# Seven block products for eight in the second quarter of the last network's first half

## The chip, the cores and the metric

The kernel runs on one core of a Trainium2 chip. The metric is the time of one execution in device microseconds, here the median of three. The engines are named as in the profile: PE is TensorE's matrix multiplication (PEld its weight load), DVE is VectorE, ACT is ScalarE, POOL is GpSimd, SP is SyncE.

## The reference

Attention over windows of 128 positions with a linear bias gives x (1152 tokens of 512 elements). Four networks of experts follow, weighted by domain probabilities, and then one network of 2048 hidden elements with a squared relu:

```python
scores = scale * np.matmul(q, k.transpose(0, 1, 3, 2))      # masked to a window of 128, with bias
attn_out = softmax(scores) @ v
x = attn_out, heads side by side                            # 1152 x 512

for e in range(4):                                          # w1: 4 x 512 x 1024, w2: 4 x 1024 x 512
    h = np.maximum(x @ w1[e], 0.0)
    out += p[:, e:e + 1] * (h @ w2[e])

x = out
h = np.maximum(x @ w_in, 0.0)                               # w_in: 512 x 2048
return h * h @ w_out                                        # w_out: 2048 x 512
```

## The kernel before

Every product of two f32 matrices is computed from high and low parts (xh, xl for x; wh, wl for weights): three matmuls, high by high, high by low and low by high. TensorE does all the products, the other engines make the parts.

The kernel counts six networks. Numbers 0 to 3 are the experts; the last network is cut into two halves of 1024 hidden elements, number 4 (`E`) and number 5. Each of them has four groups g of 256 hidden elements, and each group two weight loads: index 2 x (4 e + g) for the first matrix, plus one for the second. Two groups make what is called a quarter below: r = 0 is network 4's first quarter, r = 2 its second.

Work goes in items, in the order of the list `items`. There are two sorts. A **single** item (lines 1155 and 1186 of the code, matmuls on L939 and L1166) takes one of three chunks of 384 tokens and one tile of 128 hidden elements: 12 matmuls of 384 columns for gemm1. Four tiles make a stage of 48. Their gemm2 takes 36 matmuls per chunk, three row tiles of 12. A **pair** item (`gemm1_pair`, matmuls on L1053; gemm2 on L1131) takes a pair of chunks of tokens (2 x 256 or 2 x 320, `PAIRS`) and a group of 256 hidden elements, cuts x, weights and result into two by two blocks and computes the four blocks of the result from seven block products in place of eight, so with 42 matmuls. That needs sums of blocks: of weights (`w_forms`: wsum on L356, ha, hs, la, ls; 11 POOL operations, where hi and lo parts need 4) and of x (`x_forms`: t1, t2, m4, t3 for each pair of chunks, 14 DVE operations on L975 and 4 roundings on ACT, L1006, in two work tiles fxwork). The sums t3 go back into the place of xh and xl, so they wait until single items have read those (`x_free`).

A pair's seven products use three accumulators, pa, pb, pc. Group 2 writes pb, DVE adds it to the copy p1 into u2, group 5 goes on in pb and gives u3; c12, c21 and c22 follow, then the squared relu r (for networks 4 and 5) and its parts hmem. For single items of these networks the squared relu is r on L1152 (DVE, after ACT's L1151), hmem on L1153 and POOL's remainder on L500.

Networks 1 to 3 are pairs throughout; network 4 is single throughout; network 5 is pairs. Network 4 begins by turning the experts' sum into the new x by transposes (`to_x2`, L1201), tile by tile.

The last network's weights come as 64-bit numbers and are converted during the middle networks (`convert`): each load is taken in two halves, and a half is an ACT absolute value (L271), a DVE clamp (L277) and shift (L284) and two DVE joins (L291) on tiles wconv and wraw, then a store to memory (L251) and the next load (L239), both on ACT's queue. In `convert` these are a list of closures; each returns False if it isn't its turn.

A planner sets the order on each engine. `fill` is called between groups of matmuls with the time that passes; it takes up to three steps of `xbg` (sums of x), up to three of `conv`, and as many weight steps of `bg` as `pace` allows. `clock` holds, per engine, how far its assumed work reaches; a step with no room is put off. `spent` adds an assumed duration, as 0.85 for a POOL operation of a weight form. The engines then run their lists strictly in order.

Of the kernel before, what the change touches and what calls it, by code (L numbers as in the profile page):

```python
# [130 lines left out]
def kernel(  # L131
# [14 lines left out]
    nc = tc.nc  # L146
# [76 lines left out]
    def convert():  # L223
# [10 lines left out]
        def load(j, eng):  # L234
            i, h = todo[j]
            src, nk, nf = w_src(*order[i])
            raw[j] = places[j % 2][0]
            m = nk // 2
            eng.dma_start(  # L239
                out=raw[j].rearrange("p (k f) t -> p k (f t)", k=m).bitcast(mybir.dt.int64),  # L240
                in_=src[:, h * m:(h + 1) * m, :],
            )
            at["raw", j] = clock["now"] + 7.0

        def swap(j):
# [9 lines left out]

        def reload(j):
            if not by(at["out", j]):
                return False
            load(j + 2, nc.scalar)

        def steps(j):
# [3 lines left out]
            def begin():  # L265
                if not (by(at["raw", j]) and by(at.get(("gone", j - 2), 0.0))):
                    return False
# [20 lines left out]
            def join(part, amount, op):  # L288
# [6 lines left out]
                at["out", j] = clock["DVE"] + 0.5  # L295
# [5 lines left out]
            if j + 2 < len(todo):  # L301
                ops.append(lambda: reload(j))
            if j:
                ops.insert(1, lambda: swap(j - 1))
            if j + 1 == len(todo):
                ops += [lambda: swap(j), lambda: (fxkeep.append(places[0]), fxkeep.append(places[1]),
                                                  free.append(buf))[-1]]
            return ops
# [29 lines left out]
    def w_forms(i):  # L338
# [30 lines left out]
        def part_lo(o, src):  # L369
# [4 lines left out]
            spent("POOL", 0.85)  # L374
# [8 lines left out]
        def done(o):  # L383
# [7 lines left out]
            spent("POOL", 0.85)  # L391
# [19 lines left out]
    def w_ops(i):  # L411
# [24 lines left out]
        def lo(o):  # L436
# [4 lines left out]
            spent("POOL", 0.85)  # L441
# [592 lines left out]
    def remainder(out, x, y, n, lag):  # L1034
# [4 lines left out]
        spent(eng, 0.15 + (0.0024 if eng == "POOL" else 0.0014) * n, lag)  # L1039
# [131 lines left out]
    def evac(e, ch, tiles, f=0, two=False):  # L1171
        c0 = PAIRS[ch][0] if two else chunks(e)[ch][0]
        for i, y in tiles:
            nt = c0 // P + i
            if e == 0 or (e == E and f < FT // 2):
# [3 lines left out]
            spent("ACT" if e == E and f < FT // 2 else "DVE", 0.74, 1.38 if two else 0.69)  # L1179
# [8 lines left out]
            elif e == E and f < FT // 2:  # L1188
                nc.scalar.activation(out=yt, in_=y, func=ACTF.Copy)
            elif e == E:  # L1190
                nc.vector.tensor_tensor(out=yt, in0=y, in1=yt, op=ALU.add)
# [40 lines left out]
    for e in range(1, NE):  # L1232
        for r in range(0, NQ, 2):
            if e == E:
# [97 lines left out]
    def fill(share, us, need=0.0):  # L1332
# [24 lines left out]
    def pace(it):  # L1357
# [8 lines left out]
        return max(most * step, len(bg) / 2)  # L1366
# [296 lines left out]
    fxwork, fxbuf, fxkeep, x_late, conv = [], [], [], [], []  # L1663
# [13 lines left out]
    def want(i):  # L1677

        clock["force"] = True
        while i not in ready:  # L1680
            bg_run()
            if i not in ready:
                loads()
                while wnext["load"] == wnext["ops"] and conv:
                    assert conv.pop(0)() is not False
                    loads()
# [4 lines left out]
    for it, (e, ch, f, two) in list(enumerate(items))[N1:]:  # L1691
# [8 lines left out]
        if e >= E and (ch or f):  # L1700
            run_x2("y")
        quota["n"] = pace(it)
# [6 lines left out]
        else:  # L1709
# [20 lines left out]
        if (e, f) in ((0, FT - 1), (E, FT - 1)) and not two:  # L1730
# [6 lines left out]
        last = not two and (e, ch, f) in ((0, len(CHUNKS0) - 1, FT - 1), (E, len(CHUNKS) - 1, FT - 1))  # L1737
# [37 lines left out]
```

## Time and profile before

| | |
|---|---|
| median of three runs | 669.87 us (669.85 to 670.09) |
| the profiled execution | 669.66 us |
| its span | 667.8 us |
| PE busy | 657.0 us (98%) |
| DVE, ACT, POOL busy | 477.3, 316.9, 388.7 us |

The span is the part of the execution between the first and the last instruction that the profiler saw; 1.86 us lie outside it. Times in the trace are microseconds from the span's start. A row of the timeline gives start, duration (the sum of both where it says x2), engine, line, operation, what is written and read, and in brackets the engine's idle time ahead of it with what ended it. Matmuls are pipelined: each row shows 0.28 us and more, and the next begins 0.12 us after it for 256 columns.

### The profile page before, as it was taken

Reading aid. Unit: us, or ns where it says so; the run is one execution under the profiler, and the core shown is the slowest. Engines: PE = TensorE matmul, PEld = TensorE weight load, DVE = VectorE, ACT = ScalarE, POOL = GpSimd, SP = SyncE. Lnnn points to the kernel's source line nnn. Section 1 sums busy time; section 2 is a strip of 40 time slices with the busy share of each in tenths; the row PEclk is TensorE's granted clock in tenths of the full one; section 3 lists DMA queues with packets and bytes.
Section 4 is the critical chain, followed back from the end, with each engine's and each line's share of the span. In section 5 each row is a group of like instructions: output and inputs, shape, how many; then the busy total and the mean of one; then the engine's idle time right before and its main releaser. Section 6 shows DMA issues by size and latency. Waiting matters only on the chain.

```text
span 667.8 us, 10929 instructions
## 1 busy us (share of the span) xinstructions
PE 657.0 (98%) x3892; PEld 586.9 (88%) x3892; DVE 477.3 (71%) x983; ACT 316.9 (47%) x765; POOL 388.7 (58%) x468
## 2 busy tenths in 40 slices
PE   8999999999999999999999999999999999999997
PEld 7788788889889899898989999898999999898996
DVE  5799997847878877777877876876668744545453
ACT  7898787623534433334343443333464534333120
POOL 4588886536957744653654554331458984856331
PEclk9999999999999999999999999999999999999999
DMA  9943232010413444344335245354122001100012
GB/s 239 260 116 83 66 84 62 11 64 31 158 32 111 141 143 121 117 128 152 116 127 158 79 147 170 118 166 147 60 95 79 1 1 63 64 1 1 0 64 79
DMA packets 44022, 64.42 MB, mean 96 GB/s; under 512 B 4160, under 2 KB 26176, under 8 KB 43968
## 3 DMA queue, kind: packets, MB, share of 16 engines
q1 hardware_dynamic: 32704, 39.35, 19.3%
q10 hardware_dynamic: 11264, 24.38, 12.2%
q8 instruction: 30, 0.49, 0.3%
q14 instruction: 24, 0.20, 0.1%
HBM read 52.97 MB, written 10.75 MB: 95 GB/s over the span
## 4 chain that ended last, share of the span: by engine, by line
PE 87%; DVE 5%; ACT 3%; POOL 2%; issue 1%; DMA 1%; SPq 0%; POOLq 0%
PE yacc L1131 29%; PE hps L1053 26%; PE yacc L1166 13%; PE hps L939 12%; PE xps L733 2%; PE tp L861 1%; POOL ts L849 1%; PE sc L813 1%; DVE ts L825 1%; DVE khl L500 1%; ACT ts L834 1%; DMA first<-in_qT_dram 1%; DVE pt L500 1%; PE xtp L1201 1%; DVE fxwork L975 1%
## 5 line engine op out<-in xcount | busy, mean ns | idle before, releaser
L1131 PE MATMUL yacc<-wh,hmem 128*128 128x512 f32 x576 | 183.7, 390 | 0.0
L500 POOL TENSOR_TENSOR wl<-wraw,wh 128x256 fp32r<-128x256 f32 (+1 forms) x107 | 103.8, 994 | 63.8 <-ACT wh L433 51.2
L1131 PEld LDWEIGHTS yacc<-wh,hmem 128*128 128x128 f32 x576 | 108.2, 188 | 21.7
L1131 PE MATMUL yacc<-wl,hmem 128*128 128x512 f32 x288 | 112.4, 390 | 0.0
L1166 PE MATMUL yacc<-wh,hmem 128*128 128x512 f32 x272 | 89.3, 393 | 0.0
L500 POOL TENSOR_TENSOR ls<-wsum,hs 128x256 fp32r<-128x256 f32 x64 | 54.5, 879 | 48.1 <-ACT hs L380 47.6
L1064 ACT ACTIVATE p<-hps 128x256 f32<-128x256 f32 (+1 forms) x64 | 26.2, 410 | 98.7 <-PE hps L1053 98.2
L939 PE MATMUL hps<-xh,wh 128*128 128x384 f32 (+1 forms) x208 | 66.8, 321 | 0.4 <-DVE xl L500 0.4
L939 PE MATMUL hps<-xh,wl 128*128 128x384 f32 (+1 forms) x208 | 65.5, 315 | 0.0
L939 PE MATMUL hps<-xl,wh 128*128 128x384 f32 (+1 forms) x208 | 65.4, 314 | 0.0
L1068 DVE TENSOR_TENSOR u<-hps,p 128x256 f32<-128x256 f32 (+1 forms) x64 | 29.1, 455 | 50.1 <-PE hps L1053 50.0
L1131 PEld LDWEIGHTS yacc<-wl,hmem 128*128 128x128 f32 x288 | 54.1, 188 | 10.0
L1166 PEld LDWEIGHTS yacc<-wh,hmem 128*128 128x128 f32 x272 | 51.0, 188 | 10.4
L291 DVE SCALAR_TENSOR_TENSOR wconv<-wraw,wconv 128x512 int32<-128x512 int32 x64 | 57.2, 893 | 1.3
L1088 ACT ACTIVATE hmem<-c 128x256 fp32r<-128x256 f32 (+1 forms) x72 | 31.0, 445 | 54.0 <-DVE c L1068 52.8
L500 POOL TENSOR_TENSOR la<-wraw,ha 128x256 fp32r<-128x256 f32 x48 | 44.4, 948 | 20.0 <-ACT ha L366 20.0
L849 POOL TENSOR_SCALAR ts<-ts,st 128x256 f32<-128x256 f32 (+2 forms) x80 | 40.1, 514 | 24.7 <-DVE st L844 14.2
L1166 PE MATMUL yacc<-wl,hmem 128*128 128x512 f32 x136 | 53.2, 391 | 0.0
L500 POOL TENSOR_TENSOR hmem<-c,hmem 128x256 fp32r<-128x256 f32 (+1 forms) x32 | 26.9, 859 | 38.4 <-ACT hmem L1084 38.4
L500 POOL TENSOR_TENSOR hmem<-r,hmem 128x384 fp32r<-128x384 f32 x24 | 26.2, 1094 | 39.1 <-ACT hmem L1153 39.1
L1089 DVE SCALAR_TENSOR_TENSOR hmem<-c,hmem 128x256 fp32r<-128x256 f32 (+1 forms) x72 | 38.5, 555 | 14.6 <-ACT hmem L1088 13.3
L834 ACT ACTIVATE ts<-ts,st 128x256 f32<-128x256 f32 (+2 forms) x80 | 37.1, 467 | 8.4 <-DVE st L825 8.2
(138 smaller groups left out, 1748.7 us busy)
## 6 DMA issues: line engine op xcount, KB each, us to landing
wraw<-in_w_dram SPq DMA_DIRECT2D x32, 512.0 KB, 3.8
wraw<-in_w_out_dram ACTq DMA_DIRECT2D x16, 512.0 KB, 3.8
w<-wconv ACTq DMA_DIRECT2D x32, 256.0 KB, 4.1
wraw<-w SPq DMA_DIRECT2D x16, 512.0 KB, 3.4
wraw<-in_w_in_dram ACTq DMA_DIRECT2D x14, 512.0 KB, 4.0
rq<-in_qT_dram SPq DMA_DIRECT2D x8, 256.0 KB, 6.8
out_dram<-y SPq DMA_DIRECT2D x8, 256.0 KB, 2.1
rk<-in_kT_dram SPq DMA_DIRECT2D x8, 192.0 KB, 4.9
```

What stands on the lines that cost most here:

```text
L291: nc.vector.scalar_tensor_tensor(out=ai, in0=raw[j][:, :, part], scalar=amount, in1=ai, op0=op, op1=ALU.bitwise_or,)
L500: e.tensor_tensor(out=out, in0=in0, in1=f32(in1), op=ALU.subtract)
L834: nc.scalar.activation(out=ts[0:n, g, :], in_=ts[0:n, g, :], func=ACTF.Exp, bias=st[0:n, 0, g:g + 1], scale=-1.0, accum_out=st[0:n, 1, g:g ...
L849: nc.gpsimd.tensor_scalar(out=ts[0:n, g, :], in0=ts[0:n, g, :], scalar1=st[0:n, 2, g:g + 1], scalar2=1.0, op0=ALU.mult, op1=ALU.mult,)
L939: nc.tensor.matmul(out=ps, lhsT=l_[:, k, cs], rhs=r_[:, k, cols], start=(k == 0 and r_ is xh and l_ is wh and not second), stop=(k == KT - ...
L1053: nc.tensor.matmul(out=ps, lhsT=a[l_][:, k, :], rhs=b[r_][:, k, :], start=start and k == 0 and l_ == r_, stop=stop and k == 1 and l_ == 1, ...
L1064: nc.scalar.activation(out=out, in_=x, func=ACTF.Copy)
L1068: nc.vector.tensor_tensor(out=out, in0=x, in1=y, op=ALU.add)
L1088: nc.scalar.activation(out=hh, in_=src, func=ACTF.Relu)
L1089: nc.vector.scalar_tensor_tensor(out=hl, in0=src, scalar=0.0, in1=f32(hh), op0=ALU.max, op1=ALU.subtract)
L1131: nc.tensor.matmul(out=y, lhsT=l_[:, ns], rhs=r_[:, fo, :], start=(first and fo == 0 and j == 0), stop=(last and fo == FTQ - 1 and j == 2),)
L1166: nc.tensor.matmul(out=y, lhsT=l_[:, ns], rhs=r_[:, fo, :], start=(first and j == 0), stop=(last and j == 2),)
```

## The change

Network 4's second quarter becomes pair items: 24 items of singles for r = 2 were the rule for all of network 4, and now hold for r = 0 alone. Four things go with it. The sums of the new x are started during network 4's first quarter, one pair of chunks at a time, and two transposes of x are run per item. The place t3 comes free at the end of the first quarter. The evacuation that begins a y is that of the first quarter in either sort of item (`fresh`). And the first weights of groups 2 and 3 of network 4 are turned by `w_forms`.

Beside that, the conversion's store and next load go from its list of steps to a list `moves` of their own, from which `fill` takes one per call; the conversion runs only where no sums of x are due, and its buffers are freed at its end. A POOL operation of a weight form is counted at 0.97 in place of 0.85 while sums of x are due, a remainder at 0.0026 per column in place of 0.0024, and `pace` asks for all of the last weights' steps instead of half.

```diff
@@ convert
-        def swap(j):
+        def move(j):
             i, h = todo[j]
             if not by(at["out", j]):
                 return False
...
             if h:
                 stored.add(i)
-
-        def reload(j):
-            if not by(at["out", j]):
-                return False
-            load(j + 2, nc.scalar)
+            if j + 2 < len(todo):
+                load(j + 2, nc.scalar)
...
-                at["out", j] = clock["DVE"] + 0.5
+                if part == 0:
+                    at["out", j] = clock["DVE"] + 0.5
+                    moves.append(lambda: move(j))
...
-            if j + 2 < len(todo):
-                ops.append(lambda: reload(j))
-            if j:
-                ops.insert(1, lambda: swap(j - 1))
...
@@ w_forms, w_ops (four places)
-            t["end"] = spent("POOL", 0.85)
+            t["end"] = spent("POOL", 0.97 if xbg else 0.85)
...
@@ remainder
-        spent(eng, 0.15 + (0.0024 if eng == "POOL" else 0.0014) * n, lag)
+        spent(eng, 0.15 + ((0.0026 if xbg else 0.0024) if eng == "POOL" else 0.0014) * n, lag)
...
@@ evac
-            if e == 0 or (e == E and f < FT // 2):
+            fresh = e == E and f < (NQ if two else FT) // 2
+            if e == 0 or fresh:
...
@@ items
-            if e == E:
+            if (e, r) == (E, 0):
                 fs = range(r * FTQ, (r + 2) * FTQ)
                 items += [(e, ch, f, False) for ch in range(len(CHUNKS)) for f in fs]
             else:
...
@@ fill
+        if moves and moves[0]() is not False:
+            moves.pop(0)
         for _ in range(3):
-            if conv and need and (x_late or not xbg) and conv_due[0] >= 1.0 and conv[0]() is not False:
+            if conv and need and not xbg and conv_due[0] >= 1.0 and conv[0]() is not False:
...
@@ pace
-        return max(most * step, len(bg) / 2)
+        return max(most * step, len(bg) / (1 if wnext["ops"] == len(order) else 2))
...
@@ the loop over items
         if e >= E and (ch or f):
             run_x2("y")
+            run_x2("y")
...
-            if e == E and not x2todo and not x_late and (fxkeep or len(free) > 4):
-                fxbuf[:] = [x[1] for x in fxkeep]
-                fx_room()
-                x_late.append(1)
-                (x0_most, x0_last), (x1_most, x1_last) = x_forms(0, "DVE"), x_forms(1, "DVE")
-                xbg += x0_most + x1_most + x0_last + x1_last
-                xbg.append(lambda: free.extend(fxbuf))
-                x_rest = [len(x1_last) + 1]
+            if e == E and len(x_late) < 2 and len(x2todo) in (0, 5) and (x_late or len(free) > 2):
+                c = len(x_late)
+                if c == 0:
+                    fx_room()
+                x_late.append(x_forms(c, "DVE"))
+                if c == 1:
+                    (x0_most, x0_last), (x1_most, x1_last) = x_late
+                    xbg += x1_most + x0_last + x1_last
+                    xbg.append(lambda: (free.extend(fxbuf), fxbuf.clear()))
+                    x_rest = [len(x1_last) + 1]
+                else:
+                    xbg += x_late[0][0]
...
-        if (e, f) in ((0, FT - 1), (E, FT - 1)) and not two:
+        if (e, f) in ((0, FT - 1), (E, FT // 2 - 1)) and not two:
             x_free[0] = sum(chunks(e)[ch])
```

The order on DVE where single items end and the first pair of the last network begins. In the kernel before this is the start of network 5 (r is the squared relu of a single item, y an evacuation, fxwork and xl sums of x and their remainder, u and c the pair's sums):

```order
773 L1152 TENSOR_TENSOR r<-hps,r 128x384 x4
774 L975 TENSOR_TENSOR xl<-fxwork,xh 128x2x256
775 L975 TENSOR_TENSOR fxwork<-xh 128x640
776 L975 TENSOR_TENSOR fxwork<-fxwork,xl 128x640 x2
777 L1191 TENSOR_TENSOR y<-yacc,y 128x512 x3
778 L1152 TENSOR_TENSOR r<-hps,r 128x384 x4
779 L975 TENSOR_TENSOR xl<-fxwork,xh 128x2x320
780 L1068 TENSOR_TENSOR u_6323<-hps,p_6321 128x256
781 L1068 TENSOR_TENSOR u_6324<-hps,p_6321 128x256
```

In the changed kernel it is the start of network 4's second quarter (wconv is the conversion's tile; line numbers are three higher, or one in the conversion):

```order
757 L978 TENSOR_TENSOR xl<-fxwork,xh 128x2x256
758 L1155 TENSOR_TENSOR r<-hps,r 128x384
759 L978 TENSOR_TENSOR fxwork<-xh 128x640
760 L1155 TENSOR_TENSOR r<-hps,r 128x384
761 L978 TENSOR_TENSOR fxwork<-fxwork,xl 128x640
762 L1155 TENSOR_TENSOR r<-hps,r 128x384
763 L978 TENSOR_TENSOR fxwork<-fxwork,xl 128x640
764 L978 TENSOR_TENSOR xl<-fxwork,xh 128x2x320
765 L292 SCALAR_TENSOR_TENSOR wconv<-wraw_2417,wconv 128x512 x2
766 L1071 TENSOR_TENSOR u_5902<-hps,p_5900 128x256
767 L1071 TENSOR_TENSOR u_5903<-hps,p_5900 128x256
```

One operation stood between the last r and the first u before; now a sum, its remainder and two joins stand there.

The order on DVE at the second pair, before (network 5):

```order
787 L1078 SCALAR_TENSOR_TENSOR c_6326<-c_6326 128x256
788 L1078 SCALAR_TENSOR_TENSOR c_6327<-c_6327 128x256
789 L1191 TENSOR_TENSOR y<-yacc,y 128x512 x3
790 L1068 TENSOR_TENSOR u_6450<-hps,p_6448 128x256
791 L1068 TENSOR_TENSOR u_6451<-hps,p_6448 128x256
```

and of the change (network 4):

```order
773 L1081 SCALAR_TENSOR_TENSOR c_5905<-c_5905 128x256
774 L1081 SCALAR_TENSOR_TENSOR c_5906<-c_5906 128x256
775 L278 TENSOR_SCALAR wconv<-wconv 128x512
776 L285 TENSOR_SCALAR wconv<-wconv 128x512
777 L292 SCALAR_TENSOR_TENSOR wconv<-wraw_2418,wconv 128x512 x2
778 L278 TENSOR_SCALAR wconv<-wconv 128x512
779 L285 TENSOR_SCALAR wconv<-wconv 128x512
780 L292 SCALAR_TENSOR_TENSOR wconv<-wraw_2417,wconv 128x512 x2
781 L1071 TENSOR_TENSOR u_6039<-hps,p_6037 128x256
```

Two halves of the conversion have come between the first pair's last c and the second pair's u; the evacuations of y there are ACT's now.

The order on POOL in the same place, before (the middle of network 4, whose following items are single):

```order
180 L500 TENSOR_TENSOR hmem<-r,hmem 128x384
181 L356 TENSOR_TENSOR wsum<-wsum,wraw 128x256
182 L356 TENSOR_TENSOR wsum<-wraw 128x256
183 L356 TENSOR_TENSOR wsum<-wraw,wsum 128x256
184 L500 TENSOR_TENSOR la<-wraw,ha 128x256 x3
185 L500 TENSOR_TENSOR ls<-wsum,hs 128x256 x4
186 L500 TENSOR_TENSOR hmem<-r,hmem 128x384 x3
```

and of the change:

```order
186 L503 TENSOR_TENSOR hmem<-r,hmem 128x384
187 L359 TENSOR_TENSOR wsum<-wraw 128x256
188 L359 TENSOR_TENSOR wsum<-wraw,wsum 128x256
189 L503 TENSOR_TENSOR la<-wraw,ha 128x256 x3
190 L503 TENSOR_TENSOR hmem<-c_5906,hmem 128x256
191 L503 TENSOR_TENSOR ls<-wsum,hs 128x256
192 L503 TENSOR_TENSOR hmem<-c_5904,hmem 128x256
193 L503 TENSOR_TENSOR hmem<-c_5905,hmem 128x256
194 L503 TENSOR_TENSOR hmem<-c_5906,hmem 128x256
195 L503 TENSOR_TENSOR ls<-wsum,hs 128x256 x3
196 L503 TENSOR_TENSOR wl<-wraw,wh 128x256 x4
```

The weight form for a group has the same operations as before in this place, but the ls now stand between and behind the remainders hmem of the pair.

## Rows read from the trace of the kernel before

**Rows 1.** the page: busy time of the engines, and TensorE's granted clock in tenths

```profile
PE 657.0 (98%) x3892; PEld 586.9 (88%) x3892; DVE 477.3 (71%) x983; ACT 316.9 (47%) x765; POOL 388.7 (58%) x468
...
PEclk9999999999999999999999999999999999999999
```

**Rows 2.** stages: start:end us, length, busy of PE, PEld, DVE, ACT, POOL; granted clock

```profile
519.72:536.26 16.54, 16.54 (x86) 15.04 (x84) 11.50 (x14) 8.42 (x17) 15.61 (x16) 1.00 0.00 1
...
552.80:563.23 10.43, 10.43 (x58) 10.04 (x57) 3.12 (x6) 5.12 (x11) 3.15 (x4) 1.00 0.10 26
...
sum 95.41, PE 95.41 PEld 87.56 DVE 61.13 ACT 46.93 POOL 64.43; mean PE 23.85 PEld 21.89 DVE 15.28 ACT 11.73 POOL 16.11
```

**Rows 3.** the chain of waits: start us, length, what

```profile
519.88 8.34 PE hps L939 x48
...
563.39 5.09 PE hps L1053 x42
568.49 6.15 PE yacc L1166 x27
...
579.73 5.47 PE yacc L1131 x24
585.19 6.16 PE hps L1053 x42
```

**Rows 4.** timeline of DVE, first pair of network 1

```profile
176.26 1.25 DVE L975 TENSOR_TENSOR fxwork<-xh,fxwork 128x640 f32<-128x640 f32 x1
177.54 1.25 DVE L975 TENSOR_TENSOR fxwork<-fxwork,xl 128x640 f32<-128x640 f32 x1
178.71 0.41 DVE L1068 TENSOR_TENSOR u<-hps,p 128x256 f32<-128x256 f32 x1
```

**Rows 5.** timeline of PE: that pair, and a single stage's start

```profile
175.76 0.28 PE L1053 MATMUL hps<-xh,ha 128*128 128x256 f32 x1
...
179.18 0.38 PE L1053 MATMUL hps<-xh,hs 128*128 128x256 f32 x1 [0.39 <-DVE u L1068]
...
503.17 0.33 PE L939 MATMUL hps<-xh,wh 128*128 128x384 f32 x1
```

**Rows 6.** timeline of DVE, end of network 4's first quarter

```profile
500.65 0.96 DVE L277 TENSOR_SCALAR wconv<-wconv 128x512 f32<-128x512 f32 x1
...
502.53 2.26 DVE L291 SCALAR_TENSOR_TENSOR wconv<-wraw,wconv 128x512 int32<-128x512 int32 x2
...
512.95 0.56 DVE L1152 TENSOR_TENSOR r<-hps,r 128x384 f32<-128x384 f32 x1 [0.95 <-ACT r L1151]
513.42 0.83 DVE L975 TENSOR_TENSOR fxwork<-xh 128x640 f32<-128x640 f32 x1
514.29 2.83 DVE L975 TENSOR_TENSOR fxwork<-fxwork,xl 128x640 f32<-128x640 f32 x2
```

**Rows 7.** timeline of ACT, start of network 5

```profile
562.96 0.72 ACT L1006 ACTIVATE xh<-fxwork 128x640 fp32r<-128x640 f32 x1
```

**Rows 8.** timeline of DVE: conversion where POOL is idle or nearly so

```profile
266.86 1.41 DVE L291 SCALAR_TENSOR_TENSOR wconv<-wraw,wconv 128x512 int32<-128x512 int32 x2
...
290.31 0.43 DVE L277 TENSOR_SCALAR wconv<-wconv 128x512 f32<-128x512 f32 x1 [0.28 <-ACT wconv L271]
290.77 0.43 DVE L284 TENSOR_SCALAR wconv<-wconv 128x512 int32<-128x512 int32 x1
```

**Rows 9.** timeline of DVE, first pair of network 5

```profile
563.71 1.11 DVE L975 TENSOR_TENSOR xl<-fxwork,xh 128x640 fp32r<-128x640 f32 x1 [1.22 <-ACT xh L1006]
...
570.83 0.75 DVE L1078 SCALAR_TENSOR_TENSOR c<-c 128x256 f32<-128x256 f32 x2
```

**Rows 10.** timeline of POOL, end of network 4's first quarter

```profile
512.84 0.73 POOL L356 TENSOR_TENSOR wsum<-wraw 128x256 f32<-128x256 f32 x1
...
515.11 1.32 POOL L356 TENSOR_TENSOR wsum<-wsum,wraw 128x256 f32<-128x256 f32 x1
...
518.96 3.88 POOL L500 TENSOR_TENSOR la<-wraw,ha 128x256 fp32r<-128x256 f32 x3
```

More of the change, by code (lines that the diff above doesn't have):

```diff
@@ L242, in load @@
             )
-            at["raw", j] = clock["now"] + 7.0
-        def swap(j):
+            at["raw", j] = clock["now"] + 5.0
+        def move(j):
             i, h = todo[j]
@@ L265, in begin @@
             def begin():
-                if not (by(at["raw", j]) and by(at.get(("gone", j - 2), 0.0))):
+                while moves and clock["force"]:
+                    moves.pop(0)()
+                if ("raw", j) not in at or not by(at["raw", j]):
+                    return False
+                if j > 1 and not by(at["gone", j - 2]):
                     return False
@@ L294, in join, with leave @@
                 )
-                at["out", j] = clock["DVE"] + 0.5
+                if part == 0:
+                    at["out", j] = clock["DVE"] + 0.5
+                    moves.append(lambda: move(j))
+            def leave():
+                while moves and clock["force"]:
+                    moves.pop(0)()
+                if moves:
+                    return False
+                free.extend([buf] + [x[1] for x in places])
             ops = [
@@ L300, in steps @@
             ]
-            if j + 2 < len(todo):
-                ops.append(lambda: reload(j))
-            if j:
-                ops.insert(1, lambda: swap(j - 1))
[L305 to L308, printed above, removed]
+            return ops + [leave] if j + 1 == len(todo) else ops
         for j in range(len(todo)):
@@ L373, in part_lo @@
             rest("POOL", t["la"][0][:, js, :], src, t["ha"][0][:, js, :])
-            spent("POOL", 0.85)
+            spent("POOL", 0.97 if xbg else 0.85)
         def round_s(o):
@@ L390, in done @@
             rest("POOL", t["ls"][0][:, js, :], t["s"][:, js, :], t["hs"][0][:, js, :])
-            spent("POOL", 0.85)
+            spent("POOL", 0.97 if xbg else 0.85)
             if o == 6:
@@ L1178, in evac @@
             yt = ytile[nt]
-            spent("ACT" if e == E and f < FT // 2 else "DVE", 0.74, 1.38 if two else 0.69)
+            spent("ACT" if fresh else "DVE", 0.74, 1.38 if two else 0.69)
             if e == 0:
@@ L1187, in evac @@
                 )
-            elif e == E and f < FT // 2:
+            elif fresh:
                 nc.scalar.activation(out=yt, in_=y, func=ACTF.Copy)
-            elif e == E:
-                nc.vector.tensor_tensor(out=yt, in0=y, in1=yt, op=ALU.add)
             else:
@@ L1662 @@
     attn_close()
-    fxwork, fxbuf, fxkeep, x_late, conv = [], [], [], [], []
+    fxwork, fxbuf, moves, x_late, conv = [], [], [], [], []
     conv_due = [0.0]
@@ L1685, in want @@
                     assert conv.pop(0)() is not False
+                    while moves:
+                        moves.pop(0)()
                     loads()
@@ L1736 @@
             fill(1.0, 2.1, 3.0)
-        last = not two and (e, ch, f) in ((0, len(CHUNKS0) - 1, FT - 1), (E, len(CHUNKS) - 1, FT - 1))
+        last = not two and (e, ch, f) in ((0, len(CHUNKS0) - 1, FT - 1), (E, len(CHUNKS) - 1, FT // 2 - 1))
         left = LAG if last else (1, len(pend), len(pend), 0)[f % 4] if not two else 1
```

2 lines of the change are left out of this document (1 added, 1 removed).

## The prediction

> **What bounds the kernel now.** I read the page first: TensorE is busy for 657.0 of 667.8 us, and the clock granted to it is the upper of its two levels nearly everywhere [rows 1]. The kernel gets shorter by TensorE work that goes, and longer by every wait that TensorE then meets. Next the table of busy time by stage, cut at the first matmul of each gemm1 stage of network 4's second quarter: TensorE has no gap in 95.41 us, VectorE is busy for 61.13 of them and GpSimd for 64.43; in the stage from 519.72 GpSimd is busy for 15.61 of 16.54 us [rows 2]. So there is spare time on the two helpers over the whole stretch, but not in each piece of it. Last the chain of waits, which runs through matmuls alone here and so prices each stage [rows 3], and the rows of the one place before where pairs follow upon single tiles with sums of x still to be made, the start of network 1 [rows 4, 5].
>
> **The gain.** The second quarter of network 4 has three single stages of gemm1, 48 matmuls of 384 columns each: 3 x 8.34 = 25.02 us (the first of the three in [rows 3]). They become four pair stages of 42 matmuls, like those of network 5's first quarter: two of 256 columns at 5.09 and two of 320 at 6.16, 22.50 us in sum (one of each in [rows 3]). That removes **2.52 us** of TensorE's time. gemm2 keeps its 108 matmuls, and the evacuations and the output are the same; these terms are nothing.
>
> **The wait at the first pair.** In a pair, group 5 of the seven products writes the accumulator of group 2 again, so it waits for VectorE's u, which reads that accumulator. u stands in VectorE's queue behind what was put ahead of it. In network 1 two sums of x (176.26, 177.54) stood there, and u ended at 179.12: the matmul that was due 24 matmuls after the pair's first (175.76 plus 24 x 5.09/42 = 2.91, so 178.67) began at 179.18 [rows 3 to 5]. In the changed kernel five operations stand between the last relu square r and the first u: a sum of x, its remainder xl (with ScalarE's rounding between), and two joins of the conversion.
> The pair would begin 10.43 us after the single stage that starts at 503.17, as network 5's does behind its own [rows 2, 5], at 513.60, and group 5 is due at 516.51. The last r ended at 513.51 there [rows 6]. From then, with GpSimd idle: sum 0.83 (at 513.42 in [rows 6]), rounding 0.72 [rows 7], remainder 0.83 again, two joins 1.41 [rows 8], u 0.42: 517.72, and 0.06 to the matmul. Group 5 is 1.27 us late; an r that is 0.3 earlier makes it 1.0. Beside GpSimd: sum 1.25 [rows 4], rounding 0.72, remainder 1.11 [rows 9], two joins 2.26 (at 502.53 in [rows 6]), u 0.42: 519.33 with the matmul, 2.8 us late; with the 1.42 that the sums beside GpSimd took at 514.29 it is 3.0 or a little over. GpSimd's list has the weight sums and the la remainders in just this place, as before, where they filled 512.84 to 522.84 [rows 10]. I take **2.5 us**, nearer to the upper end, and keep 1.0 and 3.0.
> ScalarE gives a second reason why the lower end is not reached easily: the roundings hs of the weights wait there for GpSimd's four sums, the last of which had ended by 518.96 before [rows 10], and they stand ahead of the copy p5 that group 6 waits for (due at 517.2). At GpSimd's pace of 1.32 a sum, with one remainder of r less in between, that is 1.5 us or so; it lies inside the 2.5 and is not added.
>
> **The wait at the second pair.** Behind the first pair's last c stand two whole halves of the conversion (clamp, shift, two joins each) and then the second pair's u. In network 5 the last c ended at 571.58, 8.35 us after its pair began [rows 2, 9]; here that is 513.60 + 2.5 + 8.35 = 524.45. The second pair's group 5 is due at 513.60 + 2.5 + 5.09 + 6.15 (nine gemm2 matmuls in each of three tiles) + 2.91 = 530.25 [rows 3]. Two halves with GpSimd idle are 2 x (0.43 + 0.43 + 1.41) = 4.54 [rows 8] and u with its matmul 0.48: 529.5, in time. Beside GpSimd one half took 500.65 to 504.79, 4.14 us [rows 6]: two end at 532.73, the matmul begins at 533.2, 2.95 us late. GpSimd has three ls, four wl and a weight sum listed there, some 6 us alone, but part of it waits for ScalarE; so I take the middle of the conversion's 4.54 and 8.28, 6.4, which makes the matmul 1.1 late: **1.2 us** with the rounding copies and stores that ScalarE has in between, ends 0 and 2.95. At the third pair gemm2 gives 5.47 us more before the next u and fewer conversion operations stand there: nothing.
>
> **Edits that cost nothing.** The store and the next load of the conversion go from its list of steps to one of their own. Both stay on ScalarE's queue, and a store waits for a join there; what is queued behind it is the copy p1, which the u above needs, but VectorE is still busy with the other half by then. If that cover goes, it is part of the 2.95. In the middle networks the conversion's steps then stand in other gaps, never more than five ahead of a u, as before; TensorE has no wait there now, and I bound this by 0.3 us either way. The second transposes of x per item and the chunk-wise start of the sums fall among single tiles, where VectorE has 2.1 us per tile for an r of 0.56 [rows 6] and a sum or two. The remaining weight forms (11 GpSimd operations for 4, twice) must be ready for pair two: the last ls that it needs would end about 1 us before. At network 5's start the sums of x are gone now, but there was no wait to save. GpSimd's assumed 0.97 instead of 0.85 and the other figures only move orders.
>
> **Sum.** -2.52 + 2.5 + 1.2 = +1.2 on the profiled execution's 669.66 gives 670.8. The median is 0.21 above that execution, so **671.0**.
>
> **Rivals.** (a) Faster: GpSimd's operations fall into other gaps, the waits are 1.0 and 0: 669.87 - 1.5 = 668.4, and 667.4 if none is left. For it: VectorE is free for a third of the stretch [rows 2]. Against: the five operations ahead of u are late even alone. Chance 0.18.
> (b) Slower: the two halves ahead of the second u run beside GpSimd, and so does the first stretch. With both in full the waits are 3.0 and 2.95 and the time 669.87 - 2.52 + 5.95 = 673.3; it decides from a second wait of 1.5 on, 671.9. For it: GpSimd's 15.61 of 16.54 [rows 2]. Chance 0.27.
> (c) Slower still, by exclusion: where a VectorE operation on two SBUF operands and a GpSimd operation could not overlap at all, each sum would cost 0.83 + 0.73 (GpSimd's alone at 512.84 [rows 10]) = 1.56 and each join 1.43. First wait: 513.51 + 2 x 1.56 + 0.72 + 2.86 + 0.48 = 520.69, 4.2 late; second: two halves of 3.72, 2.1 late; in sum 669.87 - 2.5 + 6.3 = 673.7. The rows speak against it: beside GpSimd's 1.32 us sums the sums of x took 1.25 to 1.42, not 1.56, and both engines' rows stretch at once [rows 4, 6, 10]. Chance 0.07.
> This is what the Trainium skill, page "SBUF — State Buffer", section "SBUF: two separate sides", states: the port pair that VectorE and GpSimd share is an exclusive lock, held for the whole instruction, and the other engine blocks. By it the time would be (c)'s 673.7 instead of 671.0; this trace agrees that they hinder each other, not that one stands still.
> (d) The change does not do what it says for the second pair, because an ls of GpSimd comes after it is needed: margin 1 us, price up to 1 us on top, 671 to 672. Chance 0.05.
>
> **How the numbers follow.** Forecast (waits of 2 to 3 and 0.5 to 1.5: 669.9 to 671.9) 0.43, (b) 0.27, (a) 0.18, (c) 0.07, (d) 0.05. A measurement of this kernel can tell about 0.2%, 1.34 us, from no change: 668.5 to 671.2 is "same". (a) lies below for nearly all of its chance: faster 0.17. Of the forecast 0.37 lies within, and with the edges of (a), (b) and (d) it makes 0.43; slower has the rest, 0.40. The range reaches from a second wait of nothing (668.3) to nearly both in full (672.9); left out are the case without any wait, the top of (b), and (c).
>
> **What would show it.** Right: TensorE's gemm1 of the second quarter in pieces of about 5.1 and 6.2 us plus a gap of 2 to 3 us between matmuls 24 and 25 of its first pair, released by VectorE's u; a second gap there of about 1 us in its second pair; joins of over 1 us just ahead of these u. Wrong: no gap, or one released by ScalarE's p5 or by ls; gaps in networks 1 to 3, which would put the conversion's new order at fault; a granted clock that falls behind a gap, which no row here prices; or waits in network 5, whose weights GpSimd makes after this.

## The result and the profile after

| | before | after |
|---|---|---|
| median | 669.86 us (669.85 to 670.09, 6 runs) | 674.4 us (673.8 to 675.71, 6 runs) |
| profiled execution, its span | 669.66, 667.8 us | 674.09, 672.2 us |

The changed kernel is slower: the ratio is 1.0066, 95% interval 1.0055 to 1.0077, or 4.5 us. The prediction was 671.0, range 668.3 to 672.9.

On the page, TensorE's granted clock still reads 9 in every slice as in [rows 1], and TensorE's busy time has barely moved (one core; busy us, share of the span, instructions):

```profile
PE 658.0 (98%) x3916; PEld 586.4 (87%) x3916; DVE 491.3 (73%) x1007; ACT 315.6 (47%) x773; POOL 391.3 (58%) x486
...
PEclk9999999999999999999999999999999999999999
```

The table of stages, as in [rows 2], cut at the pairs of network 4's second quarter, shows where it goes (start:end, length, busy of PE, PEld, DVE, ACT, POOL, granted clock, DMA share, GB/s):

```profile
514.18:519.47 5.29, 3.03 (x25) 2.83 (x24) 4.40 (x5) 3.12 (x8) 5.29 (x5) 1.00 0.37 136
519.47:522.81 3.34, 3.34 (x19) 3.34 (x19) 1.74 (x4) 0.69 (x2) 2.62 (x5) 0.63 0.23 80
522.81:529.44 6.63, 6.63 (x29) 5.40 (x28) 6.28 (x9) 3.86 (x8) 5.49 (x7) 0.93 0.27 81
529.44:540.78 11.34, 10.81 (x68) 9.65 (x66) 8.77 (x14) 4.83 (x12) 9.82 (x12) 1.00 0.52 185
540.78:553.50 12.72, 11.87 (x67) 10.65 (x66) 9.68 (x15) 5.11 (x11) 6.75 (x8) 1.00 0.17 63
```

The first pair's gemm1 begins at 514.18, stands still for 2.3 us, and then runs for three us at a granted clock of 0.63 of full speed: its matmuls fall from the upper level (2.4 GHz) to the lower (1.2 GHz). The later gaps are smaller. The list of who waited for whom after 470 us (total, times, longest) has four waits of TensorE where the kernel before had none:

```profile
PE hps L1056 <- DVE u L1071: 2.8, 2, 2.3
PE hps L1056 <- ACT p L1067: 1.1, 2, 0.9
```

The first of them in the timelines, DVE and PE, to be read beside [rows 4, 6]:

```profile
513.66 0.89 DVE L978 TENSOR_TENSOR fxwork<-fxwork,xl 128x640 f32<-128x640 f32 x1
515.36 1.45 DVE L978 TENSOR_TENSOR xl<-fxwork,xh 128x640 fp32r<-128x640 f32 x1 [0.80 <-ACT xh L1009]
516.73 2.35 DVE L292 SCALAR_TENSOR_TENSOR wconv<-wraw,wconv 128x512 int32<-128x512 int32 x2
519.01 0.41 DVE L1071 TENSOR_TENSOR u<-hps,p 128x256 f32<-128x256 f32 x1
```

```profile
519.47 0.39 PE L1056 MATMUL hps<-xh,hs 128*128 128x256 f32 x1 [2.26 <-DVE u L1071]
...
522.60 0.41 PE L1056 MATMUL hps<-hm,la 128*128 128x256 f32 x1
```

A matmul of 256 columns shows 0.28 us at the upper level and 0.41 at the lower. Two figures are given for a wait below. The idle time stands in the row's brackets, here 2.26 us. How late the matmul is, counted from when it was due at the pair's own pace (24 matmuls after the pair's first), is some 0.16 more, here 2.42, because a row shows 0.28 us and the next begins 0.12 after it.

The account of the two profiled spans: each stage against the same stage without waits, 5.09 and 6.16 us for gemm1 and 6.15 for 27 matmuls of gemm2 [rows 3].

| | us |
|---|---|
| network 4 starts later (468.41 for 467.82; 0.1 of it is there at the stage at 144.6) | +0.6 |
| three single stages (twelve items, where the text on the change says 24) become four pair stages | -2.5 |
| first pair, wait for u and slow stretch (8.63 for 5.09) | +3.5 |
| gemm2 behind it, begun at the lower level (6.63 for 6.15) | +0.5 |
| second pair, wait for u (5.87 for 5.09) | +0.8 |
| third pair, wait for p (7.26 for 6.16) | +1.1 |
| network 5's first pair, wait for p (5.59 for 5.09) | +0.5 |
| sum; the spans differ by 4.4 | +4.5 |

### The profile page after: what moved, and what is told of

Same layout as the page of the kernel before. It is cut to its first block, busy times and chain, and to the rows that moved or that the text cites. A ratio compares the mean times of both kernels' runs of the same rounds, so it can differ in the third digit from the quotient of the medians.

```text
span 672.2 us, 11028 instructions
## 1 busy us (share of the span) xinstructions
PE 658.0 (98%) x3916; PEld 586.4 (87%) x3916; DVE 491.3 (73%) x1007; ACT 315.6 (47%) x773; POOL 391.3 (58%) x486
## 4 chain that ended last, share of the span: by engine, by line
PE 81%; DVE 7%; POOL 4%; ACT 4%; issue 2%; DMA 1%; SPq 0%; POOLq 0%; ACTq 0%
PE yacc L1134 29%; PE hps L1056 27%; PE yacc L1169 9%; PE hps L942 8%; PE xps L736 2%; PE tp L864 2%; PE sc L816 1%; POOL hmem L503 1%; ACT ts L837 1%; POOL ts L852 1%; DVE ts L828 1%; DMA first<-in_qT_dram 1%; POOL wsum L359 1%; DVE wconv L292 1%; PE xtp L1203 1%
## 5 line engine op out<-in xcount | busy, mean ns | idle before, releaser
L503 POOL TENSOR_TENSOR wl<-wraw,wh 128x256 fp32r<-128x256 f32 (+1 forms) x99 | 91.6, 950 | 83.3 <-ACT wh L436 43.4
L1134 PE MATMUL yacc<-wl,hmem 128*128 128x512 f32 x324 | 126.4, 390 | 0.0
L503 POOL TENSOR_TENSOR ls<-wsum,hs 128x256 fp32r<-128x256 f32 x72 | 62.8, 903 | 27.0 <-ACT hs L383 26.6
L503 POOL TENSOR_TENSOR hmem<-c,hmem 128x256 fp32r<-128x256 f32 (+1 forms) x48 | 41.9, 888 | 44.7 <-ACT hmem L1087 44.7
L942 PE MATMUL hps<-xh,wh 128*128 128x256 f32 (+1 forms) x160 | 50.5, 316 | 0.3 <-DVE xl L503 0.3
L942 PE MATMUL hps<-xh,wl 128*128 128x256 f32 (+1 forms) x160 | 49.4, 309 | 0.0
L942 PE MATMUL hps<-xl,wh 128*128 128x256 f32 (+1 forms) x160 | 49.3, 308 | 0.0
L359 POOL TENSOR_TENSOR wsum<-wraw 128x256 f32<-128x256 f32 x36 | 29.5, 819 | 32.1 <-PE hps L1056 18.3
L1056 PE MATMUL hps<-xh,hs 128*128 128x256 f32 (+1 forms) x144 | 43.2, 300 | 3.0 <-DVE u L1071 3.0
L1056 PE MATMUL hps<-xh,ha 128*128 128x256 f32 (+1 forms) x144 | 42.6, 296 | 1.1 <-ACT p L1067 1.1
```

What stands on the lines that cost most here:

```text
L503: e.tensor_tensor(out=out, in0=in0, in1=f32(in1), op=ALU.subtract)
L942: nc.tensor.matmul(out=ps, lhsT=l_[:, k, cs], rhs=r_[:, k, cols], start=(k == 0 and r_ is xh and l_ is wh and not second), stop=(k == KT - ...
L1056: nc.tensor.matmul(out=ps, lhsT=a[l_][:, k, :], rhs=b[r_][:, k, :], start=start and k == 0 and l_ == r_, stop=stop and k == 1 and l_ == 1, ...
L1134: nc.tensor.matmul(out=y, lhsT=l_[:, ns], rhs=r_[:, fo, :], start=(first and fo == 0 and j == 0), stop=(last and fo == FTQ - 1 and j == 2),)
```

## The experiments

**What stands ahead of the first u.** Two kernels test this: one leaves out the two joins, one takes GpSimd's sums away beside them.

```diff
-                nc.vector.scalar_tensor_tensor(
+                if j != 28:
+                    nc.vector.scalar_tensor_tensor(
...
```

> Leaves out the two joins of the conversion that stand ahead of the first pair's u in network 4's second quarter (so one half of one weight load is not converted fully). In the changed kernel they took 516.73 to 519.01 and the matmul of group 5 began 2.42 us late. Theory A, the joins are the wait: u ends at 517.15, group 5 is 0.1 to 0.2 us late, no other gap follows, the granted clock stays at 1.00 and the time falls by 2.3 for the gap and 1.5 for the slow stretch, to about 670.6. Theory B, two doors: the copy p5 on ScalarE stands behind the second rounding hs, which waits for GpSimd's weight sums until about 518.2, so group 6 is 1.3 us late instead and the time falls to 671.9 if the clock stays up, 673.2 if it falls all the same.

It took 673.71 us (672.51 to 674.12). This is theory B's second wait, with a larger total than the 671.9 that it gave. Group 5 is 0.17 late, but group 6 is 1.07 late for p5, which stands behind a rounding that waits for GpSimd's sums:

```profile
519.05 0.63 ACT L384 ACTIVATE hs<-wsum 128x512 fp32r<-128x512 f32 x1 [1.46 <-POOL wsum L360]
519.59 0.36 ACT L1068 ACTIVATE p<-hps 128x256 f32<-128x256 f32 x1
```

In the pairs the clock stayed at the upper level, and the second pair now waited 1.71 us for its u, in place of 0.68. That I had not expected: what the first pair gains the second partly loses, because VectorE's next two halves of the conversion do not move up as far.

About 0.9 us of the profiled execution comes from somewhere else. The granted clock is low at its very start, which this edit does not touch: the page reads 7 in the first slice, where the changed kernel has 9.

```profile
PEclk7999999999999999999999999999999999999999
```

The stage after the attention, at 144.75 in the changed kernel, begins at 145.63 here. From that stage to the end the profile has 525.93 us for the changed kernel's 527.43, so in the profiles the two joins are worth 1.5 and not only the 0.7 between the medians. The next kernel's profile has the same start (145.65).

```diff
-            nc.gpsimd.tensor_tensor(out=t["s"][:, o:o + 2, :], in0=x(), in1=y(), op=op)
+            if (e, g) == (E, NQ - 1):
+                nc.scalar.activation(out=t["s"][:, o:o + 2, :], in_=x(), func=ACTF.Copy)
+            else:
+                nc.gpsimd.tensor_tensor(out=t["s"][:, o:o + 2, :], in0=x(), in1=y(), op=op)
...
+                nc.sync.dma_start(out=t["la"][0][:, js, :].bitcast(F32), in_=src)
```

> For the second group of network 4's second quarter GpSimd's four weight sums are replaced by copies on ScalarE and its three low parts by copies on SyncE's queue (their values are not the sums, so that group's result is another), so that GpSimd has only the remainders of r beside VectorE from 511 to 521 us. Theory A, GpSimd stretches what stands ahead of u: the last remainder xl takes 0.83 for 1.45 and the two joins 1.41 for 2.35, u ends near 518.0 and group 5 is 1.0 us late for 2.42. If a gap of 1.0 leaves the granted clock at 1.00 the time falls by 1.4 + 1.5 to 671.5; if the clock falls after it too, 673.0. Rival, the order alone makes the wait: gap of 2 us or more, 674.

It took 673.61 us (672.64 to 674.79). These are the same VectorE operations, with GpSimd idle from 516.9 on:

```profile
516.77 0.82 DVE L984 TENSOR_TENSOR xl<-fxwork,xh 128x640 fp32r<-128x640 f32 x1 [0.81 <-ACT xh L1015]
517.52 1.41 DVE L292 SCALAR_TENSOR_TENSOR wconv<-wraw,wconv 128x512 int32<-128x512 int32 x2
518.85 0.42 DVE L1077 TENSOR_TENSOR u<-hps,p 128x256 f32<-128x256 f32 x1
```

So GpSimd's share is 0.63 of xl's 1.45 and 0.94 of the joins' 2.35. The gap fell from 2.42 to 1.29 (0.73 for p, which my copies on ScalarE delayed, and 0.56 for u), and the clock stayed up in the pairs. The total fell by 0.8 and not by 2.9 (by 1.3 from the stage after the attention on, 526.09 us): the second pair's wait grew to 2.02.

**The third pair's wait.**

```diff
-            nc.scalar.dma_start(out=single[i][:, h * n:(h + 1) * n], in_=both[:, j % 2, :])
+            (nc.sync if j == 31 else nc.scalar).dma_start(
+                out=single[i][:, h * n:(h + 1) * n], in_=both[:, j % 2, :]
+            )
```

> The store of the conversion's last half is issued on SyncE instead of ScalarE. In the changed kernel it is issued at 543.51, after the joins end, and the copy p at 543.94 stands behind it; TensorE waits 1.01 us for p in the third pair. Theory A, the queue: p comes at about 541.8 instead, u still ends at about 543.9 behind the joins, which is before group 5 is due (544.3), the gap goes and the time falls by 1.1 us to 673.3. Rival: u waits for the joins anyway and the gap only moves from p to u: within 0.2 us of the change.

It took 672.94 us (672.88 to 673.0), 1.5 less. The third pair's gemm1 took 6.15 us for 7.26 and has no wait, which is 1.1 of it. In the changed kernel ScalarE's queue reads as follows: the store is held until the joins end at 543.48, and p stands behind it:

```profile
543.51 0.33 ACTq L251 DMA_DIRECT2D w<-wconv  x1
543.94 0.77 ACT L1067 ACTIVATE p<-hps 128x320 f32<-128x320 f32 x2 [4.54 <-PE hps L1056]
```

With the store elsewhere it reads:

```profile
541.90 0.44 ACT L1069 ACTIVATE p<-hps 128x320 f32<-128x320 f32 x1 [2.49 <-PE hps L1058]
```

This kernel's profile also tells what the lower clock cost. Its first gap is the same (2.43 late), and the clock stayed at the upper level:

```profile
514.36:521.96 7.60, 5.33 (x44) 5.12 (x43) 5.66 (x9) 3.81 (x9) 6.89 (x8) 1.00 0.32 109
521.96:528.10 6.14, 6.14 (x29) 5.07 (x28) 5.74 (x9) 3.74 (x8) 5.33 (x7) 1.00 0.41 131
528.10:535.30 7.20, 5.35 (x43) 5.13 (x42) 5.99 (x10) 3.00 (x8) 6.49 (x8) 1.00 0.31 109
```

From the first pair's start to the second gemm2 it took 20.94 us; the changed kernel took 8.63 + 6.63 + 5.87 = 21.13. The 1.5 us that the slow stretch takes come back but for 0.2, since the second u ends at 532.9 in both: VectorE's list sets that, and a slower TensorE only waits less for it. Two waits of 2.43 and 2.01 are what the two pairs pay at the upper level. In the changed kernel the second is 0.68. The matmul behind that u begins at the same time in both (the changed kernel first):

```profile
532.99 0.39 PE L1056 MATMUL hps<-xh,hs 128*128 128x256 f32 x1 [0.53 <-DVE u L1071]
...
532.99 0.39 PE L1058 MATMUL hps<-xh,hs 128*128 128x256 f32 x1 [1.85 <-DVE u L1073]
```

**Which edit of the change brings the waits.** In this kernel the block products alone are undone and all other edits kept:

```diff
-            if (e, r) == (E, 0):
+            if e == E:
...
-        if (e, f) in ((0, FT - 1), (E, FT // 2 - 1)) and not two:
+        if (e, f) in ((0, FT - 1), (E, FT - 1)) and not two:
...
```

> Undoes the block products alone: the second quarter of network 4 is single items again, all other edits stay. Theory A: the edits to the conversion's list and to the counts cost the 0.58 us by which network 4 began later (two waits for u in network 1's third pair instead of its first, and about 0.1 us at one pair of each network where a pair of joins now stands ahead of u3), so 670.4, with no gap over 0.5 us after 470 us. Rival: these 0.58 come from the pairs' effect on the planner ahead of them (a weight form in place of a split), and this kernel is at 669.9.

It took 675.76 us (675.11 to 678.02): both theories fell. Without the block products the change costs 5.7 us against the 670.02 of the kernel before beside it, more than with them. The waits are the same two, at network 5's first pairs now:

```profile
PE hps L1056 <- DVE u L1071: 3.2, 2, 2.0
```

So the edits beside the pairs cost time without the pairs too. It does not follow that the pairs are free under the conversion's old rule, and the next kernel shows that they are not. The next two take the conversion's new rule from both sides. First comes the changed kernel without it:

```diff
-            if conv and need and not xbg and conv_due[0] >= 1.0 and conv[0]() is not False:
+            if conv and need and (x_late or not xbg) and conv_due[0] >= 1.0 and conv[0]() is not False:
```

> The changed kernel with one edit undone: the conversion may again run while sums of the new x are due, as in the kernel before. Theory A, VectorE's whole list ahead of the first pair's u is the bound: the conversion is done before, but nine sums of x now stand in a row between the last r and that u, at 0.8 to 1.3 us each, so TensorE waits 6 to 9 us there, and none of the later waits of 2.0, 1.1 us is left: 675 to 679. Rival, the place of the conversion alone was the fault: no wait over 1 us and 670.

It took 678.25 us (677.7 to 679.93). There is one wait of 7.34, for p behind a rounding of the sums; the sums stand in a row to the u that ends at 524.73, and no later pair waits more than 0.3. Theory A holds: the sums and the conversion together do not fit ahead of the first pair, in either order. Then comes the kernel before with the rule:

```diff
-            if conv and need and (x_late or not xbg) and conv_due[0] >= 1.0 and conv[0]() is not False:
+            if conv and need and not xbg and conv_due[0] >= 1.0 and conv[0]() is not False:
```

> The kernel before with one edit of the change: the conversion waits until no sums of x are due. One and a half halves of the conversion then come behind the sums, two joins of them ahead of the u of network 5's first pair. Theory A: those joins (1.4 to 2.3 us) behind the last remainder xl make group 5 of that pair wait 0.7 to 1.5 us, the second pair waits for 0.5 at most, so 670.6 to 671.9. Rival: single items leave VectorE enough time ahead and the time is 669.9.

It took 671.46 us (671.06 to 672.85), ratio 1.0028 (1.0018 to 1.0037). There is one wait of 1.39 us, at the pair and for the u that theory A named.

Two smaller edits follow. The first is the list for the store and the load:

```diff
-            at["raw", j] = clock["now"] + 7.0
-
-        def swap(j):
+            at["raw", j] = clock["now"] + 5.0
+
+        def move(j):
...
+        if moves and moves[0]() is not False:
+            moves.pop(0)
```

> The kernel before with one edit of the change: the conversion's store and next load in a list of their own. Theory A: this alone puts two joins between u2 and u3 in one pair of each middle network and costs the 0.5 us by which network 4 began later: 670.3 to 670.5, and nothing after 470. Rival: the 0.5 us come from elsewhere, 669.9.

It took 671.25 us (670.62 to 672.67), ratio 1.0019 (1.0009 to 1.003). All of it comes ahead of network 4, and it is more than the 0.5 expected: from the stage at 144.6 to network 4 it takes 324.50 us in the profiles, 323.18 before and 323.66 in the changed kernel. The assumed time of a load, 5.0 for 7.0, goes with the list here, so the two are not told apart. The waits for u ahead of 470 us are three:

```profile
PE hps L1058 <- DVE u L1073: 1.0, 3, 0.4
```

The second is the assumed durations, with the share of the last weights' steps:

```diff
-            spent("POOL", 0.97 if xbg else 0.85)
+            spent("POOL", 0.85)
...
-        return max(most * step, len(bg) / (1 if wnext["ops"] == len(order) else 2))
+        return max(most * step, len(bg) / 2)
```

> The changed kernel with the assumed GpSimd durations (0.85, 0.0024 per column) and the share of the last weights' steps as before. Theory A: these move a few steps on ScalarE and GpSimd alone and no wait hangs on them: 674.4, within 0.6. Rival: the longer counts keep GpSimd off VectorE's sums and without them the first gap grows to 3 us: 675.5.

It took 675.03 us (674.59 to 676.08). The range overlaps that of the changed kernel (673.8 to 675.71), so the median alone does not settle it. The profile says where the counts work: without them the two waits for u in network 1's first pair are back (0.55 and 0.48, as in [rows 5] for the first), and the first gap of the second quarter is 2.42 as in the changed kernel. From the stage at 144.6 to network 4 it takes 324.25 us: the counts give back about 0.6 of what the list costs.

**The conversion held back.** These kernels leave nothing out. The conversion pauses during network 4's single items and until the first pair's u is queued, and then does at most five steps per pair:

```diff
-            if conv and need and not xbg and conv_due[0] >= 1.0 and conv[0]() is not False:
+            if conv and need and not xbg and rest5[0] > 0 and conv_due[0] >= 1.0 and conv[0]() is not False:
+                rest5[0] -= 1
...
+        if e >= E:
+            rest5[0] = 0
...
             h = gemm1_pair(e, ch, f)
+            if e >= E:
+                rest5[0] = 5
```

> The changed kernel, with the conversion at rest from the start of network 4 until the first pair's u is queued, and then at most one half of a load per pair. Nothing is left out. Theory A: group 5 of the first pair is 0.2 us late (sum and remainder of x alone are ahead of u), group 6 waits 1.1 us for p5 as where the two joins were left out, the second and third pair wait for nothing over 0.3 us, so 669.9. Rival: the weights of network 5's last groups come late, since their conversion ends some 50 us later, and TensorE waits 2 us or more after 600.

It took 669.92 us (669.84 to 671.31), as theory A had it: the waits are 0.2 and 1.07 (p5) in the first pair and 0.69 for p in network 5's. In the next kernel the weight forms are also kept from between p1 and p5, and the stores put there:

```diff
-        if moves and moves[0]() is not False:
+        if moves and (rest5[1] == 0 or need == 1.8) and moves[0]() is not False:
...
-        while quota["left"] >= 1.0 and not given:
+        while quota["left"] >= 1.0 and not given and not (rest5[1] and need == 1.8):
...
-            rest5[0] = 0
+            rest5[:] = 0, 1
```

> As the kernel in which the conversion rests, and for networks 4 and 5 also no step of a weight form or split between the copies p1 and p5, and stores of the conversion only between them (not ahead of p1). Theory A: the wait of 1.1 us for p5 goes, that of 0.5 at network 5's first pair too if its two roundings hs are no longer ahead of p: 668.4 to 668.8, faster than the kernel before. Rival: the weight forms come later by that and the second pair waits for ls, 669.5 or more.

It took 668.18 us (667.77 to 668.78, 7 runs), ratio to the kernel before 0.9973 (0.9962 to 0.9984): **faster than both**. After 470 us the list of TensorE's waits is empty, and the pair stages are (the first still 0.26 longer than 5.09):

```profile
514.05:519.40 5.35, 5.35 (x43) 5.13 (x42) 3.03 (x6) 2.96 (x7) 5.35 (x7) 1.00 0.41 146
525.53:530.62 5.09, 5.09 (x43) 5.08 (x42) 2.81 (x7) 3.31 (x9) 5.09 (x7) 1.00 0.75 243
536.09:542.25 6.16, 6.16 (x43) 6.16 (x42) 3.96 (x7) 2.71 (x6) 4.77 (x7) 1.00 0.40 128
547.72:553.88 6.16, 6.16 (x43) 6.16 (x42) 2.71 (x6) 1.78 (x4) 3.63 (x7) 1.00 0.00 0
```

Two attempts at the rest failed.

```diff
-        fill(0.6, step, 1.8)
+        fill(0.6, step, 1.8 if e >= E else 1.0)
```

> As the one before, and in networks 1 to 3 at most one join of the conversion (in place of two) stands between u2 and u3 of a pair. Theory A: the waits of 0.1 us per network and those of 0.35 and 0.46 in network 1 (0.58 us in sum before network 4 starts) go for the larger part: 0.3 to 0.6 less than that kernel, 668.0 or so. Rival: they come from the planner's other counts, and this kernel is within 0.2 of it.

It took 670.65 us (670.56 to 671.94). One join fewer ahead of u3 in some pairs put the rest of the half ahead of another u: from the stage at 144.6 to network 4 it takes 324.17 us, 0.5 more and not less. The conversion and the weights shifted with it, and network 5 waited 1.21 us for an ls. The other attempt has the conversion's old list of steps, the load's assumed time of 7.0 and nine steps per pair:

```diff
-                if part == 0:
-                    at["out", j] = clock["DVE"] + 0.5
-                    moves.append(lambda: move(j))
+                at["out", j] = clock["DVE"] + 0.5
...
+            if j:
+                ops.insert(1, lambda: swap(j - 1))
```

> As the kernel in which the conversion rests and p goes first, but with the conversion's store and next load again in its list of steps, as in the kernel before. Nothing is left out. Theory A: the list of its own cost time ahead of network 4 (the kernel before with that list alone was 1.4 us slower), so undoing it brings network 4's start forward by 0.5 us, and the time is 667.6. Rival: its later halves now end in network 5 and the weights of the last groups come late, one wait of 1 us or more after 575, 668.5 or more.

It took 674.94 us (674.56 to 675.49). Both halves of what was written are there. Network 4 is reached in 322.54 us where the faster kernel needed 323.63 (stage at 145.06 to 467.60), so the list, with its assumed load time, does cost 1.1 us; but the conversion ends too late, and one pair of network 5 waits for its weights twice (its gemm1 took 12.03 us, with a granted clock of 0.59 behind the second wait):

```profile
PE hps L1052 <- POOL la L499: 2.3, 1, 2.3
PE hps L1052 <- POOL ls L499: 1.9, 1, 1.9
```

## Why the prediction was wrong, step by step

**The gain** was right: 2.5 us, and the stages of 5.09 and 6.16 us are there wherever nothing waits.

**The wait at the first pair** was right in kind and size: 2.5 said, 2.42 measured, with the operations named (0.89, rounding, 1.45, 2.35, 0.41) and GpSimd's part of it shown by its absence. That it fits to 0.1 is luck: the sum took 0.89 where 1.25 was in the upper end and its remainder 1.45 where 1.11 was, which cancels. The second door, p5 behind hs, is real as well (1.07 once the joins are gone).

**The wait at the second pair** was the mis-sized term: 1.2 said, 2.01 with the clock up (0.68 in the changed kernel, where the slow stretch makes TensorE late as well). The two halves took 524.95 to 532.60, 7.65 us, close to the bound of 8.28 that I had from [rows 6]:

```profile
524.95 0.41 DVE L278 TENSOR_SCALAR wconv<-wconv 128x512 f32<-128x512 f32 x1
525.40 0.85 DVE L285 TENSOR_SCALAR wconv<-wconv 128x512 int32<-128x512 int32 x1
526.28 2.26 DVE L292 SCALAR_TENSOR_TENSOR wconv<-wraw,wconv 128x512 int32<-128x512 int32 x2
528.47 0.96 DVE L278 TENSOR_SCALAR wconv<-wconv 128x512 f32<-128x512 f32 x1
529.46 0.85 DVE L285 TENSOR_SCALAR wconv<-wconv 128x512 int32<-128x512 int32 x1
530.34 2.26 DVE L292 SCALAR_TENSOR_TENSOR wconv<-wraw,wconv 128x512 int32<-128x512 int32 x2
532.53 0.41 DVE L1071 TENSOR_TENSOR u<-hps,p 128x256 f32<-128x256 f32 x1
```

I had taken the middle of idle and beside, 6.4, on the thought that GpSimd would wait for ScalarE. GpSimd was busy for nearly all of it:

```profile
525.22 1.63 POOL L503 TENSOR_TENSOR hmem<-c,hmem 128x256 fp32r<-128x256 f32 x2 [1.14 <-ACT hmem L1087]
526.81 3.21 POOL L503 TENSOR_TENSOR ls<-wsum,hs 128x256 fp32r<-128x256 f32 x3
529.99 3.90 POOL L503 TENSOR_TENSOR wl<-wraw,wh 128x256 fp32r<-128x256 f32 x4
```

That is rival (b), which was to decide from a second wait of 1.5 on. Where the conversion is held back, the second pair has no wait (5.09 us). The ls of rival (d) end at 530.02, and no matmul waited for them.

**"At the third pair nothing" and "edits that cost nothing"** failed, by 1.1 and 0.5 us. I had seen that a store waits for a join on ScalarE's queue with p1 behind it, and covered it with VectorE being busy; that cover holds at the second pair alone. At the third, group 4 needs the accumulator that p leaves, and p came 2 us late. At network 5's start I looked at u alone and not at the roundings ahead of p.

**The conversion's new order**, bounded at 0.3 us, cost 0.5 between the stage at 144.6 and network 4 in this kernel, and 1.3 by itself (with the load's assumed time). The condition "TensorE has no wait there now" did not hold, since [rows 5] show a wait of 0.39 for u in network 1, and it said nothing about joins that come between u2 and u3.

**The clock** I named among what would make the prediction wrong, without a price. It fell, but its 1.5 us were hidden for all but 0.2.

In sum: 1.2 was forecast against the profiled execution and 4.4 came. The missing 3.2 are 0.8 at the second pair, 0.2 of clock, 1.1 and 0.5 from ScalarE's queue, and 0.6 ahead.

**Rival (c)** had the mechanism right and the price too high; the prediction's reading against it, that both engines' rows stretch at once, is wrong. The two engines take turns. These are GpSimd's rows beside the first u, to be read with VectorE's above:

```profile
513.83 1.32 POOL L359 TENSOR_TENSOR wsum<-wsum,wraw 128x256 f32<-128x256 f32 x1
515.11 1.02 POOL L503 TENSOR_TENSOR hmem<-r,hmem 128x384 fp32r<-128x384 f32 x1
516.09 1.32 POOL L359 TENSOR_TENSOR wsum<-wraw 128x256 f32<-128x256 f32 x1
517.37 1.17 POOL L359 TENSOR_TENSOR wsum<-wraw,wsum 128x256 f32<-128x256 f32 x1
```

The ends follow one another: VectorE's sum 514.55, GpSimd 515.15 and 516.13, VectorE's xl 516.81, GpSimd 517.41, a join, GpSimd 518.54, the other join 519.08. Each operation ends a fixed time after the one that it met on the other engine: xl 0.68 (0.82 alone), a GpSimd sum 0.60 (0.73 alone), the last join 0.54 (0.70 alone, half of 1.41). So each waits for the other to end, and saves only some 0.14 us of its own time. The records of all 64 joins of the kernel before say the same: 32 end 0.55 us after a GpSimd operation that was under way, the other 32 take 0.68 to 0.69 us as if alone. This agrees, but for the 0.14 us, with the rule of the Trainium skill (page "SBUF — State Buffer", section "SBUF: two separate sides"), by which whichever of the two starts first has the shared pair of ports for the whole instruction and the other blocks. (c) added both durations in full, 0.28 too much for each turn, and so got 4.2 us at the first pair for the 2.42 measured; what brought the time up to (c)'s 673.7 were other terms.

What the prediction had not asked is which edit put the joins there. With the conversion and the weight forms held back, 1.7 of the pairs' 2.5 us remain.

## What to carry to other kernels

Work that is moved out of one stage goes into another; before costing its waits one by one, add up what the helper must do ahead of the first consumer (here sums, conversion and roundings) and see whether it fits at the slower, side-by-side durations. Where VectorE and GpSimd are both listed full in a place, take the upper bound, not the middle: operations of the kinds above took turns here. A transfer that waits for data belongs on a queue where nothing urgent stands behind it: one store ahead of a 0.4 us copy cost 1.1 us.

## What the runs showed of the hardware

The same idle time of TensorE, 2.26 and 2.27 us before the same matmul, was followed by the lower clock level in one profile (0.63 granted from 519.47 to 522.81) and by the upper in two others (1.00; without the store on ScalarE, and with the counts as before). An idle time of 2.00 us was followed by the lower level too (0.57 granted from 582.17 to 585.80, in the kernel without the block products). Where TensorE stood idle for 0.91 us (ahead of the matmul that came 1.07 late), 1.23 (1.39 late), 1.55 (1.71 late) and 1.85 (2.01 late) no fall followed; after 7.18 us idle, in the kernel with the conversion among the sums, the granted clock was 0.54 for the next 5 us:

```profile
523.99:529.00 5.01, 5.00 (x24) 5.00 (x25) 2.21 (x6) 2.07 (x5) 0.75 (x2) 0.54 0.00 0
```

What decides between the two levels after some 2 us idle stays open.
